# Delta-rule attention and a PReLU feed-forward on one core: another order for the first two products of the second feed-forward matrix, and other places for the copies of even steps' rows

## The chip, the core and the metric

The kernel runs on one core of a Trainium2 chip. Its engines are TensorE (PE in the profile, its weight loads PEld), VectorE (DVE), ScalarE (ACT), GpSimd (POOL) and SyncE (SP, which issues DMAs). Each takes its own list of instructions, and waits on semaphores where it needs what another engine makes. The metric is the device time of one execution in microseconds; the times of a kernel are given as the median of several runs.

## The reference

A delta-rule attention over 4 batches, 8 heads, 768 tokens and 48 dimensions; its output, as 3072 tokens of 384 numbers, goes through a feed-forward block of width 2048 with a PReLU whose slope differs by column. All in 32-bit floats.

```python
k_n = k / (np.linalg.norm(k, axis=-1, keepdims=True) + 1e-06)
for t in range(S):
    kt, vt, bt = (k_n[:, :, t], v[:, :, t], beta[:, :, t, None])
    y[:, :, t] = np.einsum('bhd,bhde->bhe', q[:, :, t], state)
    v_old = np.einsum('bhde,bhd->bhe', state, kt)
    state = state + bt[:, :, :, None] * np.einsum('bhd,bhe->bhde', kt, vt - v_old)
...
x = np.ascontiguousarray(attn_out.transpose(0, 2, 1, 3)).reshape(B * S, H * D)
h = x @ w_in
g = np.maximum(h, 0.0) + alpha * np.minimum(h, 0.0)
return (g @ w_out).astype(np.float32)
```

## The kernel before

**Steps and chunks.** The tokens go in 12 chunks of 64. The attention of one chunk takes two steps, one for each pair of batches, so there are 24 steps; step n belongs to chunk n // 2. The recurrence within a chunk is solved with triangular inverses, which VectorE makes for four steps at a time by elimination (`eliminate`, a list of small pieces). The feed-forward of a chunk handles 256 tokens: the first product (`ffn_in`, line 996) takes the 2048 columns in 8 pairs of 128, six matmuls to a pair, all into one bank of PSUM; ScalarE then writes the Relu of the negated bank to `act` (line 1006), and two VectorE operations (line 1008), one for each half of the pair, turn it into the PReLU. An fp32 matmul leaves two records in the profile.

**The second product.** From chunk 2 to chunk 7 it is `ffn_out_fast`: instead of eight products of 128 x 192 blocks with eight operand tiles each, seven (Winograd's form), on sums of blocks of `act` (`operand_sums`, VectorE, line 950; the second half of them is issued during the first product, two tiles apart) and sums of blocks of the weights. Each product runs its eight tiles in a row (`product`), into the next bank that `ps_ffn` hands out. The first product, of blocks (0, 0), is copied to `u` by ScalarE (line 1084); the second is added to it by VectorE (line 1081), and so on. Tile i of the first two products is pair i of `act`, so that their last tile is the last thing that the PReLU makes. From chunk 8 on other functions are used for both products: `ffn_in_fast` (lines 1219 to 1267), in which four shared matmuls of a pair go to one bank that ScalarE copies out (line 1248) before the next pair's may be written, and `ffn_out_faster` (line 1313).

**Order of the work.** The lists of all engines are written out by hand. A step from `JOINED` (6) on is: `burst_a` (outputs and next state of the step before, the keys through the state of this one: lines 840, 857, 802 on TensorE; then on VectorE the new state, line 865, `turn_y`, line 881, and `r`, line 812, and `a_t`, line 521); a first stretch; `turn_round`; a second stretch; `burst_b` (solve and the next steps' inverses: lines 784, 827, 733; VectorE's `u`, line 831; ScalarE's copies, line 745); a third stretch. In a stretch, `weave` interleaves feed-forward pieces (a piece is one matmul of `ffn_in`, two of `ffn_out_fast`) with pieces of other lists: each list (pieces, count, start) has its pieces spread evenly from its start to the stretch's end, at equal positions the list named first goes first:

```python
    def stretch(n, blocks, share, later, *gens, soon=0.5):
        gens = [(*x, 0.0) for x in (*gens, (part(tail, n), n))]
        gens += [(part(blocks, share), share, 0.3), (each(later), len(later), soon)]
```

In odd steps from 13 on the stretches hold 12, 18 and 12 feed-forward pieces (12, 16 and 12 in steps 9 and 11). A chunk has 48 + 28 = 76, which is what two steps hold, so each chunk's second product begins in the third stretch of an odd step: chunk 3's in step 9, chunk 7's in step 17.

**Banks.** PSUM has 8 banks. Up to step 7 three pairs of them serve the attention and two single banks (`p_ffn`) the feed-forward; at step `NARROW` (8) `banks(2, 2)` makes it two pairs and four single banks (`p_ffn` and `p_more`), and `len(ffn_banks)` becomes 4.

**Turning the attention's output.** The feed-forward needs it transposed (`xts`, two buffers). From step 8 to 22 this is done without TensorE: `turn_y(n - 1)` in `burst_a(n)` transposes 32 x 32 blocks on VectorE into `z`, and `rows_y` has 16 ScalarE copies (line 894) that put the blocks' rows in place. For odd steps n - 1 all 16 go to the first stretch of step n, from 0.4 of it on; for even ones, 8 to the second and 8 to the third stretch of step n.

Of the kernel before, what the change touches and what calls it, by code (L numbers as in the profile page):

```python
# [44 lines left out]
def kernel(  # L45
# [11 lines left out]
    nc = tc.nc  # L57

    B, H, S, D = q.shape
    DM = H * D  # L60
# [14 lines left out]
    doubles, big, ffn_banks = ExitStack(), [], []  # L75
# [25 lines left out]
    def ps_ffn():  # L101
        turn[0] = (turn[0] + 1) % len(ffn_banks)
        return ffn_banks[turn[0]]
# [79 lines left out]
    def load_v(n):  # L183
        if n < N:
            v_raw[n] = work.tile([128, H, D], FP32, name="v_raw", bufs=3)
            fetch(v, n, v_raw[n])
# [298 lines left out]
    def now(pieces):  # L485
        for x in pieces:
            x()
# [561 lines left out]
    def ffn_out_fast(c):  # L1049


        gss.pop(c)
        later = operand_sums(1)
        o = [work.tile([128, DM], FP32, name="o_sb") for _ in range(2)]
        left, right_ = slice(0, DM // 2), slice(DM // 2, DM)
        u = [work.tile([128, DM // 2], FP32, name=f"u{i}", bufs=1) for i in (2, 3)]

        def product(x, w):
            p = ps_ffn()[:, 0 : DM // 2]
            for i in range(FP):  # L1060
                nc.tensor.matmul(p, x(i), w(i), start=(i == 0), stop=(i == FP - 1))  # L1061
                if i % 2 == 1:
                    next(later, None)
                    if i < FP - 1:
                        yield
            return p

        def operand(f, u):
            return lambda i: act[:, i, f, u * 128 : (u + 1) * 128]

        def sum_(x):
            return lambda i: sums[:, i, x]

        def weight(f, v):
            return lambda i: w_half[:, i, f, v]

        def w_sum_(x):
            return lambda i: w_sum(i, x)

        def add(to, x, p):  # L1080
            nc.vector.tensor_tensor(out=to, in0=x, in1=p, op=ALU.add)

        p = yield from product(operand(0, 0), weight(0, 0))
        nc.scalar.copy(u[0], p)
        yield
        p = yield from product(operand(1, 0), weight(1, 0))
        add(o[0][:, left], u[0], p)
        yield
        for _ in later:
            assert False  # L1090
        assert summed.count(0) == summed.count(1) == 4
        p = yield from product(sum_(1), w_sum_(1))
        add(u[0], u[0], p)
        yield
        p = yield from product(lambda i: act[:, i, 0, 128:256], w_sum_(2))
        add(u[1], u[0], p)
        yield
        p = yield from product(sum_(0), w_sum_(0))
        add(o[0][:, right_], u[0], p)
        add(o[1][:, right_], u[1], p)  # L1100
        yield
        p = yield from product(sum_(2), weight(1, 1))
        add(o[0][:, right_], o[0][:, right_], p)
        store(c, 0, o[0])
        yield
        p = yield from product(operand(1, 1), w_sum_(3))
        add(o[1][:, left], u[1], p)
        store(c, 1, o[1])
        yield
# [296 lines left out]
    def is_turned(n):  # L1406
        return NARROW <= n < N - 1

    def burst_a(n):

        soon, later = [], []
        if n > NARROW:
            b = asked_in.pop()
            y, z = b[:, :, G * C : G * C + WY], b[:, :, 0:WY]
        else:
            b = ps_big()
            y, z = b[:, :, 0:WY], b[:, :, WY : 2 * WY]
        if n > JOINED:
            soon += outputs(n - 1, y)
            soon += next_state(n - 1, z)  # L1420
            if is_turned(n - 1):
                soon.append(lambda: turn_y(n - 1))
            later.append(lambda: load_late(n + 1))
        if n < N:
            p = ps_big()
            y = ps_big()[:, :, 0:WY] if n < NARROW else None
            soon += through_state(n, p[:, :, 0 : G * (D + C)], y)
            if n < JOINED + 2:
                soon += between_1(n + 1, b[:, :, 2 * WY : 2 * WY + G * HB])
            if n == JOINED:  # L1430
                soon += grams(n + EARLY, big[-1][:, :, WY : WY + G * C])
                later.append(lambda: squares(n + EARLY + 1))
            later.append(lambda: load_v(n + 3))
        now(soon)
        return later

# [264 lines left out]
    n = 12  # L1701
# [199 lines left out]
    for n in range(JOINED, N):  # L1901
        if n == NARROW:
            banks(2, 2)
        fill, share = FILL.get(n, FILLS[n % 2]), PIECES_OF.get(n, TURNS[n % NJ])
        extra = [[], [], []]
        if n == JOINED:
            place(n + 1, (0,))
            extra[1] = [(weight_sums(1, 0, 3), 3)]
            extra[2] = [(weight_sums(0, 3, 4), 1)]
        elif n == JOINED + 1:  # L1910
            extra[0] = [(weight_sums(1, 3, 4), 1, 0.6), (placing(n + 1, (1, 2, 3)), PLACING)]

        later = burst_a(n)
        if is_turned(n - 1):
            if n % 2:
                rows = rows_y(n - 1)
                extra[1].append((part(rows, 8), 8))
                extra[2].append((part(rows, 8), 8))
            else:
                extra[0].append((rows_y(n - 1), 16, 0.4))  # L1920
        stretch(fill[0], blocks, share[0], later, *extra[0], *put_off)
        put_off = []
        later = turn_round(n)
        if n == JOINED:
            extra[1].append((placing(n + 1, (1, 2, 3)), PLACING))
        stretch(fill[1], blocks, share[1], later, *extra[1], soon=0.2)
        m, ends = (n + 6) // NJ, n % NJ == 2
        if ends and n > JOINED:
            for _ in blocks:
                assert False  # L1930
            place(n + 2, (0,))
        later = burst_b(n) + [lambda: scale_v(n + 1)]
        if NARROW <= n < N - 2:
            later.append(lambda: turn_q(n + 2))
        if n == JOINED:
            stretch(fill[2], blocks, share[2], later, *extra[2])
            for _ in blocks:
                assert False
            place(n + 2, (0,))
            place(n + 3, (0,))  # L1940
            blocks = eliminate(m)
        else:
            if ends:
                blocks = eliminate(m) if m < N // NJ else iter(())
            after = [(placing(n + 2, (1, 2, 3)), PLACING)]
            if n % NJ != 1:
                after.append((placing(n + 3, (0,)), 1))
            if n >= LATE:
                put_off, after = after, []
            stretch(  # L1950
                fill[2], blocks, share[2], later, *after, *extra[2], soon=0.1 if n >= LATE else 0.5
            )
# [34 lines left out]
```

## Time and profile before

| | us |
|---|---|
| median of 3 runs | 651.65 |
| lowest, highest | 651.61, 652.92 |
| the profiled execution | 652.41 |
| its span, first to last instruction | 650.69 |

The profile's times are microseconds from the start of the span. A row of a timeline has its start, its length, engine, line, operation, tiles written and read, shape and count (successive equal instructions are merged), and in brackets the time that the engine sat idle before it and what ended that. Engines are strictly ordered lists; a wait of one instruction is a wait of everything behind it on its engine. The length of a matmul is modelled: they overlap, so that a run of them is read by the distance between starts.

In 40 equal slices of the span VectorE, ScalarE and GpSimd stand so (busy tenths, 9 is 90% or more):

```
DVE  4976998967999888858978857968967668567383
ACT  5887565345453344635544634435447356354140
POOL 6001211010000000001000000000035043062250
```

Lines 996, 1061 and 1313, the feed-forward products up to chunk 7 and the second one after it, are the largest groups of TensorE; of ScalarE it is line 894 with 64.4 us in 240 copies.

### The profile page before, as it was taken

Reading aid. Unit: us, or ns where it says so; the run is one execution under the profiler, and the core shown is the slowest. Engines: PE = TensorE matmul, PEld = TensorE weight load, DVE = VectorE, ACT = ScalarE, POOL = GpSimd, SP = SyncE. Lnnn points to the kernel's source line nnn. Section 1 sums busy time; section 2 is a strip of 40 time slices with the busy share of each in tenths; the row PEclk is TensorE's granted clock in tenths of the full one; section 3 lists DMA queues with packets and bytes.
Section 4 is the critical chain, followed back from the end, with each engine's and each line's share of the span. In section 5 each row is a group of like instructions: output and inputs, shape, how many; then the busy total and the mean of one; then the engine's idle time right before and its main releaser. Section 6 shows DMA issues by size and latency. Waiting matters only on the chain.

```text
span 650.7 us, 21683 instructions
## 1 busy us (share of the span) xinstructions
PE 629.2 (97%) x9154; PEld 552.3 (85%) x9154; DVE 498.2 (77%) x1205; ACT 313.1 (48%) x824; POOL 93.3 (14%) x204
## 2 busy tenths in 40 slices
PE   6999999999999998999999999999999999999997
PEld 4688888557788987988988888988989989999997
DVE  4976998967999888858978857968967668567383
ACT  5887565345453344635544634435447356354140
POOL 6001211010000000001000000000035043062250
PEclk9999999999999999999999999999999999999999
DMA  7957835211353242242243121121220210100000
GB/s 119 297 132 167 232 68 147 62 37 37 51 79 49 45 73 34 38 71 44 37 64 50 26 48 30 31 43 28 39 54 12 50 27 3 37 2 2 25 1 25
DMA packets 145969, 39.27 MB, mean 60 GB/s; under 512 B 139040, under 2 KB 142256, under 8 KB 145872
## 3 DMA queue, kind: packets, MB, share of 16 engines
q1 hardware_dynamic: 144000, 37.40, 28.2%
q8 instruction: 72, 1.18, 0.8%
q10 hardware_dynamic: 1872, 0.49, 0.4%
q14 instruction: 25, 0.20, 0.1%
HBM read 33.14 MB, written 4.72 MB: 58 GB/s over the span
## 4 chain that ended last, share of the span: by engine, by line
PE 71%; DVE 13%; ACT 5%; SPq 4%; DMA 3%; issue 2%; POOL 1%; ACTq 0%; DVEq 0%; POOLq 0%
PE p_ffn L1061 9%; PE p_ffn L996 8%; PE p_more L1061 7%; PE p_more L1313 7%; PE p_ffn L1039 6%; PE p_more L1229 4%; PE p_more L996 4%; PE p_ffn L1313 3%; PE p_ffn L1219 3%; DVE act L1008 3%; PE p_ffn L1224 2%; SPq L153 2%; PE p_pair L733 2%; PE p_pair L1480 2%; PE p_pair L802 2%
## 5 line engine op out<-in xcount | busy, mean ns | idle before, releaser
L996 PE MATMUL p_ffn<-xt,w_in 128*128 128x256 f32 x528 | 124.1, 384 | 2.4 <-DVE act L1008 1.8
L996 PEld LDWEIGHTS p_ffn<-xt,w_in 128*128 128x128 f32 x528 | 97.4, 190 | 17.5 <-ACT wgt L718 1.6
L894 ACT COPY xt<-z 32x96 f32<-32x96 f32 x240 | 64.4, 268 | 25.7 <-DVE z L881 22.6
L996 PE MATMUL p_more<-xt,w_in 128*128 128x256 f32 x240 | 55.7, 382 | 0.0
L745 ACT COPY inv<-p_pair 32x256 f32<-32x256 f32 x40 | 14.5, 362 | 84.7 <-DVE u L831 83.9
L599 DVE TENSOR_TENSOR block<-block,prod 128x30 f32<-128x30 f32 (+9 forms) x150 | 49.8, 332 | 5.1
L1253 POOL TENSOR_TENSOR k_t<-k_t 128x128 f32<-128x128 f32 (+1 forms) x48 | 28.9, 601 | 166.6 <-ACT k_t L1248 164.0
L996 PEld LDWEIGHTS p_more<-xt,w_in 128*128 128x128 f32 x240 | 44.9, 190 | 6.3
L593 DVE TENSOR_TENSOR prod<-block 128x30 f32<-128x30 f32 (+9 forms) x150 | 48.5, 324 | 1.2
L418 POOL TENSOR_TENSOR beta_t<-beta_t,rec 128x8 f32<-128x8 f32 x24 | 6.1, 255 | 276.5 <-DVE rec L412 267.5
L1008 DVE SCALAR_TENSOR_TENSOR act<-act,al_t,p_ffn 128x256 f32<-128x256 f32 x72 | 31.2, 475 | 17.6 <-ACT act L1006 17.6
L1006 ACT ACTIVATE act<-p_ffn 128x512 f32<-128x512 f32 x36 | 21.4, 595 | 36.7 <-PE p_ffn L996 36.6
L1061 PE MATMUL p_ffn<-w_out,act 128*128 128x192 f32 x160 | 28.1, 329 | 3.1 <-DVE act L1008 3.1
L1253 POOL TENSOR_TENSOR block<-block 128x128 f32<-128x128 f32 (+1 forms) x48 | 28.0, 582 | 15.5 <-ACT block L1248 13.0
L1061 PEld LDWEIGHTS p_ffn<-w_out,act 128*128 128x128 f32 x160 | 26.2, 190 | 4.1 <-DVE act L1008 3.7
L1219 PE MATMUL p_ffn<-xt,w_in 128*128 128x256 f32 x96 | 29.3, 387 | 0.0
L831 DVE TENSOR_TENSOR u<-p_pair,wgt 128x384 f32<-128x384 f32 x24 | 13.2, 553 | 18.0 <-PE p_pair L733 17.1
L1008 DVE SCALAR_TENSOR_TENSOR act<-act,al_t,p_more 128x256 f32<-128x256 f32 x40 | 17.3, 472 | 11.7 <-ACT act L1006 11.7
L1061 PE MATMUL p_more<-w_out,act 128*128 128x192 f32 x128 | 22.5, 328 | 2.8 <-DVE act L1008 2.8
L812 DVE TENSOR_TENSOR r<-v_raw,p_pair 64x192 f32<-64x192 f32 (+1 forms) x66 | 23.3, 353 | 2.3 <-PE p_pair L802 1.2
L1061 PEld LDWEIGHTS p_more<-w_out,act 128*128 128x128 f32 x128 | 20.9, 190 | 3.5 <-DVE act L1008 3.4
L554 ACT COPY same<-right 32x256 f32<-32x256 f32 x29 | 11.7, 403 | 22.7 <-DVE right L507 19.1
(254 smaller groups left out, 1473.1 us busy)
## 6 DMA issues: line engine op xcount, KB each, us to landing
w_out<-in_moe_w_in_dram SPq DMA_DIRECT2D x10, 512.0 KB, 5.1
v_raw<-in_v_dram SPq DMA_DIRECT2D x48, 96.0 KB, 2.7
kl<-in_k_dram SPq DMA_DIRECT2D x96, 48.0 KB, 2.4
out_dram<-o_sb SPq DMA_DIRECT2D x90, 48.0 KB, 1.6
space_out<-in_moe_w_out_dram SPq DMA_DIRECT2D x11, 384.0 KB, 4.5
ke_last<-in_k_dram SPq DMA_DIRECT2D x25, 96.0 KB, 3.2
qp<-in_q_dram SPq DMA_DIRECT2D x64, 32.0 KB, 2.2
w_out<-in_moe_w_out_dram SPq DMA_DIRECT2D x5, 384.0 KB, 4.5
```

The costliest lines, as they stand in the source:

```text
L593: nc.vector.tensor_tensor(out=prod, in0=r[:, 0:j, j : j + 1].to_broadcast([128, j, n]), in1=r[:, j : j + 1, j + 1 : HB].to_broadcast([128, ...
L599: nc.vector.tensor_tensor(out=r[:, 0:j, j + 1 : HB], in0=r[:, 0:j, j + 1 : HB], in1=prod, op=ALU.add)
L812: nc.vector.tensor_tensor(out=r[to, a], in0=v_in[to, a], in1=p[own, a, :, 0:D], op=ALU.subtract)
L894: nc.scalar.copy(to[quad(r), u, bp, t], z[quad(2 * t + u), r])
L996: nc.tensor.matmul(p_h[:, i], w_in[:, t, (f + i) * 128 : (f + i + 1) * 128], xt[:, t], start=(t == 0), stop=(t == KT - 1),)
L1008: nc.vector.scalar_tensor_tensor(out=g[:, i], in0=g[:, i], scalar=al_t[:, f + i : f + i + 1], in1=p_h[:, i], op0=ALU.mult, op1=ALU.add,)
L1039: nc.tensor.matmul(p_o[u], gs[f // 2][:, f % 2, u * 128 : (u + 1) * 128], w_out[:, f], start=(f == 0), stop=(f == FT - 1),)
L1061: nc.tensor.matmul(p, x(i), w(i), start=(i == 0), stop=(i == FP - 1))
L1219: nc.tensor.matmul(p[:, f * 256 : f * 256 + 256], w(2, f), xt[:, 2], start=True, stop=False)
L1229: nc.tensor.matmul(q[:, j], a, b, start=True, stop=True)
L1253: nc.gpsimd.tensor_tensor(out=dst, in0=a, in1=b, op=ALU.add)
L1313: nc.tensor.matmul(p, x(i), w(i), start=(i == 0), stop=(i == FP - 1))
```

## The change

It has two parts. In `ffn_out_fast`, with more than two banks for the feed-forward, the first two products are opened together: six tiles of the first, six of the second, the last two of the first, its copy to `u`, the last two of the second, its addition. The banks are handed out in the same order, and the count of pieces (28) stays. `some` is `product`'s loop over a given range of tiles; it still takes a piece of `operand_sums` after each second tile. With two banks the old order remains.

In odd steps n (whose rows are those of the even step n - 1) `turn_y` is issued at the end of `burst_a`, behind the pieces of `through_state` (`r` and `a_t`), and no longer ahead of them. The 16 row copies go 6 to the first stretch from 0.5 of it on, 2 to the second and 8 to the third from 0.3 on. In even steps nothing changes.

```diff
-        def product(x, w):
-            p = ps_ffn()[:, 0 : DM // 2]
-            for i in range(FP):
+        def some(p, x, w, which):
+            for i in which:
                 nc.tensor.matmul(p, x(i), w(i), start=(i == 0), stop=(i == FP - 1))
                 if i % 2 == 1:
                     next(later, None)
                     if i < FP - 1:
                         yield
+
+        def product(x, w):
+            p = ps_ffn()[:, 0 : DM // 2]
+            yield from some(p, x, w, range(FP))
             return p
...
+        if len(ffn_banks) > 2:
+            a, b = (
+                (ps_ffn()[:, 0 : DM // 2], operand(f, 0), weight(f, 0)) for f in range(2)
+            )
+            yield from some(*a, range(FP - 2))
+            yield from some(*b, range(FP - 2))
+            yield from some(*a, range(FP - 2, FP))
+            nc.scalar.copy(u[0], a[0])
+            yield
+            yield from some(*b, range(FP - 2, FP))
+            add(o[0][:, left], u[0], b[0])
+            yield
+        else:
+            p = yield from product(operand(0, 0), weight(0, 0))
+            nc.scalar.copy(u[0], p)
+            yield
+            p = yield from product(operand(1, 0), weight(1, 0))
+            add(o[0][:, left], u[0], p)
+            yield
...
-            if is_turned(n - 1):
+            if is_turned(n - 1) and n % 2 == 0:
                 soon.append(lambda: turn_y(n - 1))
             later.append(lambda: load_late(n + 1))
         if n < N:
...
             later.append(lambda: load_v(n + 3))
+        if is_turned(n - 1) and n % 2:
+            soon.append(lambda: turn_y(n - 1))
         now(soon)
...
                 rows = rows_y(n - 1)
-                extra[1].append((part(rows, 8), 8))
-                extra[2].append((part(rows, 8), 8))
+                extra[0].append((part(rows, 6), 6, 0.5))
+                extra[1].append((part(rows, 2), 2))
+                extra[2].append((part(rows, 8), 8, 0.3))
```

More of the change, by code (lines that the diff above doesn't have):

```diff
@@ L1081, in add @@
             nc.vector.tensor_tensor(out=to, in0=x, in1=p, op=ALU.add)
[L1083 to L1088, printed above, removed]
+        if len(ffn_banks) > 2:
[17 more added lines that the diff above has]
+            yield
         for _ in later:
```

## The prediction, made before the changed kernel was built or timed

> **What bounds the kernel now.** I read the page first, then the answer for line 1061 (all matmuls of the second feed-forward product), then the timelines of TensorE, ScalarE and VectorE around each of its waits.
>
> ```profile
> PE 629.2 (97%) x9154; PEld 552.3 (85%) x9154; DVE 498.2 (77%) x1205; ACT 313.1 (48%) x824; POOL 93.3 (14%) x204
> ...
> PEclk9999999999999999999999999999999999999999
> ```
>
> From the answer for line 1061:
>
> ```profile
> L1061 PE MATMUL p_more<-w_out,act x128: 326/326/430, 225.2 to 472.2; 128*128 128x192 f32 x128
> ...
> its engine sat idle before it (us, times) until:
>   DVE act L1008: 12.9, 8
> ```
>
> TensorE sets the time: busy for 97% of the span at full granted clock, every other engine has room. So only an idle stretch of TensorE is worth anything, and line 1061 has one kind: matmuls waiting for `act`. The 12.9 counts weight loads and matmuls both; the matmuls' part, with the rows ahead of each wait (start, length, then the idle time in brackets):
>
> ```profile
> 256.02 2.44 PE L1061 MATMUL p_ffn<-w_out,act 128*128 128x192 f32 x14
> 260.72 3.19 PE L1061 MATMUL p_ffn<-w_out,act 128*128 128x192 f32 x18 [2.25 <-DVE act L1008]
> ...
> 306.22 2.44 PE L1061 MATMUL p_more<-w_out,act 128*128 128x192 f32 x14
> 309.91 0.59 PE L1061 MATMUL p_more<-w_out,act 128*128 128x192 f32 x2 [1.25 <-DVE act L1008]
> ...
> 355.42 2.44 PE L1061 MATMUL p_more<-w_out,act 128*128 128x192 f32 x14
> 359.39 3.19 PE L1061 MATMUL p_more<-w_out,act 128*128 128x192 f32 x18 [1.53 <-DVE act L1008]
> ...
> 404.42 2.44 PE L1061 MATMUL p_ffn<-w_out,act 128*128 128x192 f32 x14
> 407.68 0.59 PE L1061 MATMUL p_ffn<-w_out,act 128*128 128x192 f32 x2 [0.82 <-DVE act L1008]
> ...
> 452.25 5.36 PE L1061 MATMUL p_ffn<-w_out,act 128*128 128x192 f32 x32
> ```
>
> A matmul leaves two records. Each block is chunks 3, 4, 5, 6, 7 in turn; 14 records are operand tiles 0 to 6, and the wait is always at tile 7. Chunk 7 has none. Its 32 unbroken records give the pitch: (5.36 - 0.33) / 31 = 0.162 us. Record 15 would start 14 x 0.162 = 2.27 after the first, so the waits cost 260.72 - 256.02 - 2.27 = 2.43, then 1.42, 1.70 and 0.99: **6.54 us in all**, a little over the idle column, because a resumed matmul also loses its overlap.
>
> Why tile 7 is late, in chunk 4 (ScalarE rows, then VectorE):
>
> ```profile
> 305.58 0.73 ACT L745 COPY inv<-p_pair 32x256 f32<-32x256 f32 x2 [3.29 <-DVE u L831]
> 306.33 0.74 ACT L745 COPY mid<-p_pair 32x256 f32<-32x256 f32 x2
> 307.08 0.51 ACT L704 ACTIVATE inv<-inverse,which 128x256 f32<-128x256 f32 x1
> 307.50 0.39 ACT L707 COPY diag<-turned 128x256 f32<-128x256 f32 x1
> 307.89 0.83 ACT L894 COPY xt<-z 32x96 f32<-32x96 f32 x3
> 308.75 0.60 ACT L1006 ACTIVATE act<-p_more 128x512 f32<-128x512 f32 x1
> ...
> 305.00 0.55 DVE L831 TENSOR_TENSOR u<-p_pair,wgt 128x384 f32<-128x384 f32 x1
> 309.38 0.87 DVE L1008 SCALAR_TENSOR_TENSOR act<-act,al_t,p_more 128x256 f32<-128x256 f32 x2 [2.57 <-ACT act L1006]
> ```
>
> VectorE's `u` comes at the end of its queue, four copies of ScalarE wait for it, and the Relu of pair 7 stands behind them and three row copies. Relu, then the first of the two line-1008 operations (half of 0.87), then TensorE goes on.
>
> **Part one, the order of the products.** No instruction is added or removed. From four banks on, the first product's tiles 0 to 5 are followed by the second's 0 to 5, then 6 and 7 of each. Chunk 2 still has two banks (its first products are all `p_ffn`), so chunks 3 to 7 change. Tile 7's matmul becomes record 27 instead of 15: due 26 x 0.162 = 4.21 after the start, at 260.23, 310.43, 359.63 and 408.63, against releases at 260.72, 309.91, 359.39 and 407.68. Alone, this leaves 0.49 us in chunk 3 and nothing elsewhere. Is alternating between two open banks free? The last chunks' product (line 1313) already does it in this order:
>
> ```profile
> 545.29 4.39 PE L1313 MATMUL p_more<-w_out,act 128*128 128x192 f32 x26
> 549.87 1.24 PE L1313 MATMUL p_more<-w_out,act 128*128 128x192 f32 x6 [0.19 <-DVE act L1267]
> ```
>
> (4.39 - 0.33) / 25 = 0.162, the same pitch, so I take nothing for it; bounds 0 both ways, since the rows agree to a nanosecond. [...]
>
> The copy of `u` (line 1084) and the add behind it are issued six matmuls, about 2 us, later. What is late next is the third product's second half, which needs the second of the `sums` operations of VectorE:
>
> ```profile
> 261.81 0.69 DVE L950 TENSOR_TENSOR sums<-sums,act 128x512 f32<-128x512 f32 x1
> ...
> 266.89 1.57 PE L1061 MATMUL p_more<-more,sums 128*128 128x192 f32 x8
> ```
>
> It is ready at 262.50 and would be wanted at 266.89 - 2.4 = 264.5: 2 us to spare in the worst chunk, so no new wait there.
>
> **Part two, the copies.** Of even steps' 16 row copies, 6 go to the second half of the first stretch, 2 to the second, 8 to the third from 0.3 on; before it was 8 and 8 from the start of the second and third. By the order in which `weave` interleaves lists of these lengths, the Relu of pair 7 loses the row copies ahead of it: three in chunks 4 to 6 (0.83 us, row above), one in chunk 3. With its 0.27 less, chunk 3's release is 260.45: 0.22 us remain. Gain so far 6.54 - 0.22 = **6.32**.
>
> The price is paid in the first stretch. `turn_y` now follows `r` and `a_t` on VectorE, and the six copies wait for its `z`, with Relus queued behind them. Step 11, the worst:
>
> ```profile
> 294.41 0.58 DVE L881 STREAM_TRANSPOSE z<-y 128x384 f32<-128x384 f32 x1
> 295.02 1.09 DVE L812 TENSOR_TENSOR r<-v_raw,p_pair 128x192 f32<-128x192 f32 x3
> 296.14 0.69 DVE L521 TENSOR_TENSOR a_t<-p_pair,minus 128x512 f32<-128x512 f32 x1
> ...
> 299.03 0.86 DVE L1008 SCALAR_TENSOR_TENSOR act<-act,al_t,p_more 128x256 f32<-128x256 f32 x2
> ...
> 294.50 0.21 ACT L408 ACTIVATE norm<-norm 128x8 f32<-128x8 f32 x1
> ...
> 296.23 0.60 ACT L1006 ACTIVATE act<-p_more 128x512 f32<-128x512 f32 x1 [0.93 <-PE p_more L996]
> ```
>
> `z` would end at 296.7. Then on ScalarE: one copy (0.27), the Relu of pair 3 (0.60), five copies (1.4), two norm operations (0.45), one copy, and the Relu of pair 4 ends near 300.3. VectorE wants it at 299.03, so it falls 1.3 us behind, and carries that to `u`. TensorE does not see it directly: pair 4's bank is next written at 306.22. But chunk 4's release becomes 309.91 - 0.83 + 1.3 = 310.38 against 310.43: still covered, by a hair. In the other odd steps to 17 the same reckoning gives less, and idle time takes it up.
>
> In steps 19 and 21 it is ScalarE's copy out of the shared bank (line 1248) that stands behind five copies:
>
> ```profile
> 487.25 0.40 ACT L718 COPY wgt<-wgt 64x4 f32<-64x4 f32 x2
> 487.99 0.58 ACT L1248 COPY k_t<-p_more 128x512 f32<-128x512 f32 x1 [0.34 <-ACT wgt L718]
> ...
> 489.27 0.39 PE L1229 MATMUL p_more<-xt,w_in 128*128 128x128 f32 x2
> ...
> 486.75 0.49 PE L1229 MATMUL p_more<-xt,w_in 128*128 128x128 f32 x2 [0.57 <-ACT block L1248]
> ```
>
> It would start at 487.65 + 5 x 0.277 = 489.03 and end at 489.61; TensorE, which needs that bank at 489.27, waits some 0.4 us. The last row shows that it does wait for this copy where that is late. Twice: **-0.8**, bounds 0 and 2 x 1.39 = 2.8 (all five copies felt). Step 23 has no `wgt` copies there and just fits.
>
> In the third stretch of steps 19 and 21 copies leave the way of the Relu whose VectorE operation ends the 0.19 wait at 549.87 (and its twin): 0 to 0.35 us each with the lost overlap, I take 0.25, **+0.5**.
>
> **Sum:** 6.3 + 0.5 - 0.8 = 6.0 us. The profiled execution took 652.41 with a span of 650.69; its like after the change 646.4, span 644.7. The median of the runs, 651.65, lies 0.76 below it: **645.7**.
>
> **Rivals.**
> *The stall only moves.* VectorE, at 77%, is what was late; TensorE arriving 1 to 2.4 us earlier meets the next operation of its queue. For it: chunk 4's release comes out only 0.05 us ahead of its need. Against: the 2 us spare at `sums`, and VectorE sat idle 2.57 us while it waited for the Relu. If half of the 6.3 comes back as new waits, or step 11's lag and those like it eat two chunks' gain (1.4 + 1.7), some 3 us are left: 648.6.
> *The copies in front hold TensorE: slower.* One mechanism: ScalarE takes its queue in order, so a copy that waits for `z` holds the Relu or line-1248 copy behind it until the bank is missing on TensorE. In favour:
>
> ```profile
> L894 ACT COPY xt<-z x240: 253/268/272, 247.0 to 593.6; 32x96 f32<-32x96 f32 x120
> ...
>   DVE z L881: 22.6, 8
> ```
>
> ScalarE already stands 22.6 us in 8 waits for `z`. If in all eight odd steps the later `z` (1.09 + 0.69 = 1.8) passed to TensorE, that is 14.2 us against 6.8 gained: 659. It decides only once a Relu is more than about 5 us late (300.3 to 306.22 in step 11); I find at most 3.5.
> *The change doesn't reach the waits.* Were the bank count read before the switch to four, the old branch would run and only the copies would act: Relu 0.83 earlier, so 0.27 + 3 x 0.83 = 2.8 less 1.3 for step 11, less 0.8, plus 0.5 = 1.2 us: 650.5. Against: `p_more` is in use by line 1061 from 225.2 on, 30 us before chunk 3.
> [...]
>
> **How the numbers follow.** Forecast 0.72; the stall moves 0.16; slower by the copies 0.05; not reached 0.06; clock 0.01. The forecast's own range is 644.4 (all 6.54, twice 0.35, no price: 7.2) to 647.7 (price 2.8). With the second case the range is **644.4 to 649.2**, which leaves out about 0.15. Faster by over 0.2% (1.3 us, about what a measurement of this kernel can tell) has the first two: 0.88; within 0.2%: 0.06; slower: 0.06.
>
> **What would show it.** Right: line 1061 without waits for `act` in chunks 4, 5, 6, and at most a few tenths in chunk 3; unbroken blocks of 28 to 32 records there; the Relu of pair 7 directly behind the four line-745 copies and line 704; a new wait of some 0.4 us before line 1229 in steps 19 and 21; `z` after `a_t` in odd steps. Wrong: line 996 waiting for `act` or a bank in odd steps' first two stretches; waits before `sums`; a wait at tile 7 in chunk 4 of over 0.3 us, which would say that step 11's lag was sized too small.

## The result

| | before, us | after, us |
|---|---|---|
| median of 4 runs each | 652.24 | 647.27 |
| lowest, highest | 651.61, 652.92 | 645.59, 647.38 |
| profiled execution, its span | 652.41, 650.69 | 645.59, 643.87 |

The ratio is 0.9918, 95% interval 0.9897 to 0.9939: the change makes the kernel faster by 5.0 us in the medians, where 6.0 were predicted, and 647.27 lies in the predicted range. The change was timed twice more, on two chips, as experiments e3 and e9: 645.72 against 653.62 (ratio 0.9893, 0.9870 to 0.9916) and 646.11 against 651.70 (0.9912, 0.9897 to 0.9927). The two profiled executions lie 6.82 us apart.

### The profile page after: what moved, and what is told of

Its sections match the earlier page's. It is cut to its first block, busy times and chain, and to the rows that moved or that the text cites. A ratio compares the mean times of both kernels' runs of the same rounds, so it can differ in the third digit from the quotient of the medians.

```text
span 643.9 us, 21686 instructions
## 1 busy us (share of the span) xinstructions
PE 628.6 (98%) x9154; PEld 552.2 (86%) x9154; DVE 497.9 (77%) x1205; ACT 312.8 (49%) x824; POOL 92.5 (14%) x204
## 3 DMA queue, kind: packets, MB, share of 16 engines
q8 instruction: 72, 1.18, 0.8%
## 4 chain that ended last, share of the span: by engine, by line
PE 87%; DVE 6%; DMA 2%; ACT 1%; issue 1%; SPq 1%; POOL 1%; ACTq 0%; DVEq 0%; POOLq 0%
PE p_ffn L996 13%; PE p_ffn L1060 9%; PE p_more L996 8%; PE p_more L1329 8%; PE p_more L1060 8%; PE p_ffn L1039 7%; PE p_more L1245 4%; PE p_ffn L1329 3%; PE p_ffn L1235 3%; PE p_pair L733 2%; PE p_ffn L1240 2%; PE p_pair L802 2%; PE p_pair L840 2%; PE p_pair L1498 2%; PE p_pair L501 2%; PE p_pair L827 2%
## 5 line engine op out<-in xcount | busy, mean ns | idle before, releaser
L1283 DVE SCALAR_TENSOR_TENSOR act<-k_t,al_t,act 128x256 f32<-128x256 f32 x32 | 19.4, 645 | 3.6 <-ACT k_t L1279 3.5
```

## The profile after

From the page of the changed kernel, the busy times and the granted clock:

```profile
PE 628.6 (98%) x9154; PEld 552.2 (86%) x9154; DVE 497.9 (77%) x1205; ACT 312.8 (49%) x824; POOL 92.5 (14%) x204
...
PEclk9999999999999999999999999999999999999999
```

From the answer for line 1060 (1061 before: the matmuls of the second product):

```profile
its engine sat idle before it (us, times) until:
  DVE act L1008: 0.2, 1
```

TensorE's work is the same to 0.6 us, in a shorter span, and the 12.9 us in 8 waits for `act` have become 0.2 in one. The timeline of TensorE, at the first two products of chunks 3, 4 and 5:

```profile
255.46 5.52 PE L1060 MATMUL p_ffn<-w_out,act 128*128 128x192 f32 x32
...
303.29 2.11 PE L1060 MATMUL p_more<-w_out,act 128*128 128x192 f32 x12
305.24 2.11 PE L1060 MATMUL p_ffn<-w_out,act 128*128 128x192 f32 x12
307.19 0.84 PE L1060 MATMUL p_more<-w_out,act 128*128 128x192 f32 x4
307.87 0.81 PE L1060 MATMUL p_ffn<-w_out,act 128*128 128x192 f32 x4
...
351.76 5.36 PE L1060 MATMUL p_more<-w_out,act 128*128 128x192 f32 x32
```

Chunk 4 shows the new order as it is: 12 records of one bank, 12 of the other, 4, 4, with no bracket for idle time. Chunk 5 is as long as chunk 7 was before, which did not wait; chunk 3 is 5.52 - 5.36 = 0.16 us longer, what is left of its wait.

Why tile 7 now comes in time in chunk 4 (ScalarE, then VectorE):

```profile
303.95 0.73 ACT L745 COPY inv<-p_pair 32x256 f32<-32x256 f32 x2 [4.88 <-DVE u L831]
...
305.86 0.39 ACT L707 COPY diag<-turned 128x256 f32<-128x256 f32 x1
306.27 0.60 ACT L1006 ACTIVATE act<-p_more 128x512 f32<-128x512 f32 x1
...
306.90 0.87 DVE L1008 SCALAR_TENSOR_TENSOR act<-act,al_t,p_more 128x256 f32<-128x256 f32 x2 [1.73 <-ACT act L1006]
```

The Relu stands directly behind the copies that wait for `u`, with no row copy between. Half of the line-1008 pair ends near 306.90 + 0.87/2 = 307.34; tile 7 is due 4.21 after 303.29, at 307.50. By these rows the margin is 0.16 us.

The two kernels issue the same matmuls in the same steps, so where the time went can be read from the start of a step's first line-840 (or 784) matmul in the two timelines:

| TensorE reaches | before, us | after, us | apart | gained since the row above |
|---|---|---|---|---|
| step 9 (line 840) | 238.79 | 238.23 | -0.56 | 0.56, from the start to step 9 |
| step 10 | 265.14 | 262.21 | -2.93 | 2.37, chunk 3 |
| step 12 (line 784) | 329.37 | 324.94 | -4.43 | 1.50, chunk 4 |
| step 13 | 336.46 | 332.80 | -3.66 | -0.77, line 733 in step 12 |
| step 14 | 362.51 | 357.06 | -5.45 | 1.79, chunk 5 |
| step 16 | 410.81 | 404.26 | -6.55 | 1.10, chunk 6 |
| step 19 (line 784) | 495.11 | 488.71 | -6.40 | -0.15, line 1245 in step 19 |
| step 20 | 504.26 | 497.59 | -6.67 | 0.27, third stretch of step 19 |
| step 21 (line 784) | 541.89 | 535.36 | -6.53 | -0.14, line 1245 in step 21 |
| step 22 | 551.05 | 544.23 | -6.82 | 0.29, third stretch of step 21 |

The losses are visible in TensorE's timeline. In step 12, in the middle of a run of 32 x 32 matmuls:

```profile
326.35 0.19 PE L733 MATMUL p_pair<-inv,mid 32*32 32x32 f32 x1
327.11 0.18 PE L733 MATMUL p_pair<-inv,mid 32*32 32x32 f32 x1 [0.57 <-issue]
```

"issue" means that the engine waited for nothing that the profile shows. In step 19, TensorE's rows and then ScalarE's:

```profile
480.08 0.49 PE L1245 MATMUL p_more<-xt,w_in 128*128 128x128 f32 x2 [0.44 <-ACT block L1264]
...
482.39 0.38 PE L1240 MATMUL p_ffn<-k_t,w_in 128*128 128x128 f32 x2
482.77 0.49 PE L1245 MATMUL p_more<-xt,w_in 128*128 128x128 f32 x2
...
492.11 5.55 PE L1329 MATMUL p_more<-w_out,act 128*128 128x192 f32 x32
...
480.45 0.54 ACT L894 COPY xt<-z 32x96 f32<-32x96 f32 x2
481.00 0.40 ACT L718 COPY wgt<-wgt 64x4 f32<-64x4 f32 x2
481.41 0.83 ACT L894 COPY xt<-z 32x96 f32<-32x96 f32 x3
482.15 0.57 ACT L1264 COPY k_t<-p_more 128x512 f32<-128x512 f32 x1
```

The 0.44 is an old wait (0.57 before). The new one shows as a distance between starts: 482.77 - 482.39 = 0.38, where this pair of lines runs at 0.22 in the kernel with the old places of the copies (e1). Three copies, not five, stand between `wgt` and the copy of the bank.

## The experiments

All were timed beside the kernel before on the same chip: e1 to e4 on one (before 653.62, 17 runs), e5 to e8 on a second (652.88, 17 runs), e9 to e12 on a third (651.70, 11 runs). Diffs are against the changed kernel.

**e1: the order of the products alone**, copies and `turn_y` as before.

```diff
-            if is_turned(n - 1) and n % 2 == 0:
+            if is_turned(n - 1):
                 soon.append(lambda: turn_y(n - 1))
...
-                extra[0].append((part(rows, 6), 6, 0.5))
-                extra[1].append((part(rows, 2), 2))
-                extra[2].append((part(rows, 8), 8, 0.3))
+                extra[1].append((part(rows, 8), 8))
+                extra[2].append((part(rows, 8), 8))
```

> The new order of the first two products alone; the copies of even steps' rows and turn_y as before. Theory (the order takes the waits, by making the last tile due 12 records later): chunks 4 to 6 without a wait at the last tiles, chunk 3 with 0.49 us (release 260.72 against due 260.23 in the old clock); steps 19 and 21 keep the 0.2 us wait before the second product's last tiles and have none behind the copy of the shared bank. 6.05 us less than before, so 0.5 us more than the full change, too little to tell from it by time. Rival (the copies do it, the order only opens banks): 2 us or less below the kernel before, waits at the last tiles in chunks 3 to 6 about as before.

Measured: 646.49 us (645.00 to 649.32), ratio 0.9908 (0.9883 to 0.9934). Chunk 3's two products in TensorE's timeline:

```profile
255.36 4.39 PE L1060 MATMUL p_ffn<-w_out,act 128*128 128x192 f32 x26
260.05 1.24 PE L1060 MATMUL p_ffn<-w_out,act 128*128 128x192 f32 x6 [0.30 <-DVE act L1008]
```

The first wait is now at record 27, as the order says, and costs 260.05 - 255.36 - 4.21 = 0.48 (0.49 predicted). Chunks 4 to 7 have none. The order alone brings nearly all of the gain.

**e2: the copies alone**, the products in their old order (`ffn_out_fast` as before the change).

```diff
-        if len(ffn_banks) > 2:
...
-        else:
...
+        p = yield from product(operand(0, 0), weight(0, 0))
+        nc.scalar.copy(u[0], p)
+        yield
+        p = yield from product(operand(1, 0), weight(1, 0))
+        add(o[0][:, left], u[0], p)
+        yield
```

> The copies of even steps' rows and turn_y moved as in the change; the order of the products as before. Theory: the waits at tile 7 stay, shorter by the copies that leave the way: chunk 3 2.43 - 0.27 = 2.2 us, chunk 4 1.42 - 0.83 + 1.3 = 1.9 (longer, step 11's lag reaches it because nothing covers it now), chunk 5 0.9, chunk 6 0.2; 0.2 us waits at the shared bank in steps 19 and 21; together about 1.5 us less than before. Rival (the copies do it): 4 us or more below the kernel before, chunk 4's wait shorter than 1 us.

Measured: 650.16 us (647.61 to 652.65, 12 runs), ratio 0.9954 (0.9935 to 0.9973). TensorE's timeline at tile 7 of chunks 3, 4 and 5:

```profile
256.45 2.44 PE L1061 MATMUL p_ffn<-w_out,act 128*128 128x192 f32 x14
260.88 4.87 PE L1061 MATMUL p_ffn<-w_out,act 128*128 128x192 f32 x18 [2.00 <-DVE act L1008]
...
308.06 2.44 PE L1061 MATMUL p_more<-w_out,act 128*128 128x192 f32 x14
312.24 0.59 PE L1061 MATMUL p_more<-w_out,act 128*128 128x192 f32 x2 [1.73 <-DVE act L1008]
...
357.74 2.44 PE L1061 MATMUL p_more<-w_out,act 128*128 128x192 f32 x14
360.73 3.19 PE L1061 MATMUL p_more<-w_out,act 128*128 128x192 f32 x18 [0.55 <-DVE act L1008]
```

By starts (less 2.27) the waits are 2.16, 1.91 and 0.72, against 2.43, 1.42 and 1.70 before. The waits of chunks 3 and 5 are shorter by 0.27 and 0.98, what the copies ahead of the Relu cost (one of 0.27, three of 0.83) and a little more; chunk 4's wait is longer by 0.49, which is step 11's lag (1.3) less the three copies (0.83), 0.47. So the second part of the change has the two effects that were predicted, close to their sizes. In the times, e2 is 3.5 us below before by the medians, where some 1.5 were expected; but 12 of the 17 executions of before and only 2 of e2's 12 had a mean granted clock below 0.9985. Among the others the medians are 651.10 and 650.08, 1.0 apart.

One row was not expected: 18 records took 4.87 us and not 3.19. The windows of the same execution, whose columns are busy time of the engines, then the granted clock (before the DMA share and GB/s):

```profile
261.00:262.00 1.00, 1.00 (x4) 1.00 (x5) 0.93 (x3) 0.72 (x4) 0.00 (x0) 0.60 0.00 0
262.00:263.00 1.00, 1.00 (x4) 1.00 (x4) 0.96 (x3) 0.98 (x3) 0.00 (x0) 0.50 0.00 0
263.00:264.00 1.00, 1.00 (x5) 1.00 (x5) 1.00 (x3) 0.94 (x4) 0.00 (x0) 0.50 0.00 0
264.00:265.00 1.00, 1.00 (x6) 1.00 (x5) 0.96 (x4) 0.94 (x5) 0.00 (x0) 0.69 0.00 0
```

Directly behind the wait TensorE has half its clock: 0.40 + 0.50 + 0.50 + 0.31 = 1.71 us of clock lost in some 3.4 us, the 4.87 - 3.19 = 1.68 of the row. The profiles of before and after have no such stretch there.

**e3: the change again**, on this chip, unaltered.

> The changed kernel once more, beside the other three on the same chip, so that they are compared with it: 5 to 6.5 us below the kernel before. If the 0.6 us stop of TensorE inside line 733 near 327 us in its first profile is an accident of that execution and no part of the change, it is absent here or stands elsewhere; if it belongs to the change it stands at the same place.

Measured: 645.72 us (644.54 to 647.13), ratio 0.9893 (0.9870 to 0.9916). In its profile chunk 3 loses 0.31, and the stop of 0.58 in line 733 stands at 326.17 again. It isn't chance of one execution.

**e4: one tile left for later instead of two, and no copies in the first stretch** (`turn_y` at its old place).

```diff
-            yield from some(*a, range(FP - 2))
-            yield from some(*b, range(FP - 2))
-            yield from some(*a, range(FP - 2, FP))
+            yield from some(*a, range(FP - 1))
+            yield from some(*b, range(FP - 1))
+            yield from some(*a, range(FP - 1, FP))
...
-            yield from some(*b, range(FP - 2, FP))
+            yield from some(*b, range(FP - 1, FP))
...
-            if is_turned(n - 1) and n % 2 == 0:
+            if is_turned(n - 1):
...
-                extra[0].append((part(rows, 6), 6, 0.5))
-                extra[1].append((part(rows, 2), 2))
+                extra[1].append((part(rows, 8), 8))
```

> A version by the theory: only the last tile of the two products is left for later (due 28 records after the start instead of 26), turn_y stands as before, no copies in the first stretch of odd steps, 8 in the second, 8 in the third from 0.3 on. Theory: no wait at the last tiles in any of chunks 3 to 7 (chunk 3's 0.2 us goes too), no wait behind the shared bank at the second of its two places in steps 19 and 21 (0.17 us each go), VectorE's 1.2 us idle time in step 11 before the operation on pair 4 gone; 0.5 us below the full change, inside its noise by time, visible in the trace. Rival (the 6 early copies are needed to clear the third stretch): the Relu of pair 7 later than in the full change, waits at the last tiles come back.

Measured: 643.80 us (643.01 to 644.46), ratio 0.9864 (0.9841 to 0.9887), the fastest of this chip's five. TensorE's timeline:

```profile
255.08 5.40 PE L1060 MATMUL p_ffn<-w_out,act 128*128 128x192 f32 x32
...
478.91 0.49 PE L1245 MATMUL p_more<-xt,w_in 128*128 128x128 f32 x2 [0.57 <-ACT block L1264]
```

Chunk 3 is unbroken, and in step 19 only the old wait of before is left. The waits account for some 0.3 + 2 x 0.15 = 0.6 us of the 1.9 to e3; the rest was open until e9 to e12.

**e5: the new order in chunk 3 only, and e6: in all but chunk 3**, both with the copies of before. They ask whether chunk 3's wait, the longest, is what brings the half-clock stretch.

```diff
-        if len(ffn_banks) > 2:
+        if len(ffn_banks) > 2 and c == 3:
```

> The new order in chunk 3 alone, copies as before: only the longest wait, 2.43 us, is taken away but for 0.46. Theory (a wait of some 2 us can also bring a stretch of half clock, 3.4 us long, behind it, as in the profile of the copies alone behind the 2.0 us wait of chunk 3; it does so in most runs of the kernel before and not in all, and that is why runs differ): runs at granted clock 1.000 are 2 us below those of the kernel before; runs with a lower clock become rare, 1 or 2 in 6 against 12 in 17, so that the median falls by some 4 us. Rival (the stretches of half clock come from elsewhere, the start-up for one): the median falls by 2 us and runs below 1.000 stay as frequent as before.

```diff
-        if len(ffn_banks) > 2:
+        if len(ffn_banks) > 2 and c != 3:
```

> The new order in chunks 4 to 7, chunk 3 and the copies as before: waits of 1.42, 1.70 and 0.99 us are taken away, the one of 2.43 stays. Theory: runs at clock 1.000 are 4.1 us below those of the kernel before; lower clocks stay about as frequent as in the kernel before (2 runs in 3), a half-clock stretch standing behind chunk 3's wait near 260 us where the profile caught one. Rival (stretches of half clock are independent of chunk 3's wait): as rare as in the run with the order alone.

Measured: e5 650.29 us (648.60 to 653.37, 12 runs), ratio 0.9962 (0.9945 to 0.9978); e6 648.95 (646.43 to 650.77, 6 runs), ratio 0.9935 (0.9914 to 0.9957). In the profiles each has the waits that were left to it and no other; e6 in chunk 3:

```profile
258.30 3.19 PE L1060 MATMUL p_ffn<-w_out,act 128*128 128x192 f32 x18 [2.27 <-DVE act L1008]
```

e5's 2.6 us lie between the two theories. The mean granted clock was below 0.9985 in 3 of its 12 executions, in 4 of e6's 6, and in 10 of the 17 of before. Among the other executions e5 is 651.65 - 650.19 = 1.5 us below before (2 expected) and e6, with two such executions, 651.65 - 647.4 = 4.2 (4.1 expected). The counts agree with chunk 3's wait as a cause of such stretches, but e2, whose wait of 2.0 us was kept, has 2 of 12, and e6's own profile has none behind the 2.27. How often a wait brings one stays open.

**e7: all 16 copies in the first stretch**, from 0.4 on: the dose at which the rival "the copies in front hold TensorE" should decide.

```diff
-                extra[0].append((part(rows, 6), 6, 0.5))
-                extra[1].append((part(rows, 2), 2))
-                extra[2].append((part(rows, 8), 8, 0.3))
+                extra[0].append((part(rows, 16), 16, 0.4))
```

> The full change, but all 16 copies of an even step's rows in the first stretch from 0.4 of it on, as odd steps' have it: the dose of the slower rival. Theory (ScalarE takes its queue in order; the copies reach TensorE once what they hold up is later than its cover): waits at tile 7 of 1.3 us in chunk 3, 2.4 in chunk 4, 0.6 in chunk 5, 0.4 in chunk 6; waits behind the shared bank of 2.6 us in steps 19 and 21 and 2.4 in step 23; 11 us above the full change and 5 above the kernel before, with half-clock stretches behind the longer waits. Rival (copies in front never reach TensorE, the banks cover them): within 1 us of the full change.

Measured: 660.79 us (659.90 to 661.48, 5 runs), ratio 1.0118 (1.0098 to 1.0138): slower than before. The waits in TensorE's timeline (line 501 in steps 9, 11 and 13, tile 7 in chunk 3, then the shared bank in steps 19, 21 and 23):

```profile
252.55 0.69 PE L501 MATMUL p_pair<-k_t 48*64 48x64 f32 x32 [1.24 <-DVE k_t L478]
...
260.74 1.24 PE L1060 MATMUL p_ffn<-w_out,act 128*128 128x192 f32 x6 [0.60 <-DVE act L1008]
...
302.38 0.69 PE L501 MATMUL p_pair<-k_t 48*64 48x64 f32 x32 [2.08 <-DVE k_t L478]
...
351.89 0.69 PE L501 MATMUL p_pair<-k_t 48*64 48x64 f32 x32 [0.75 <-DVE k_t L478]
...
489.76 0.80 PE L1245 MATMUL p_more<-xt,w_in 128*128 128x128 f32 x2 [2.40 <-ACT k_t L1264]
...
540.10 0.49 PE L1245 MATMUL p_more<-xt,w_in 128*128 128x128 f32 x2 [2.41 <-ACT k_t L1264]
...
588.92 0.49 PE L1245 MATMUL p_more<-xt,w_in 128*128 128x128 f32 x2 [1.90 <-ACT k_t L1264]
```

At the shared bank the waits came where and as long as they were expected (2.6, 2.6, 2.4 against 2.40, 2.41, 1.90). In the earlier steps most of the delay came back not at tile 7 but at line 501, for which VectorE transposes `k_t` in its queue behind the delayed work. At tile 7 there is less than was expected: by the starts 0.78 us in chunk 3, 0.27 in chunk 4, none in chunk 5 and 0.41 in chunk 6 (1.3, 2.4, 0.6 and 0.4 expected). The six other waits make 10.8 us; behind the two of 2.4 us stands a half-clock stretch each, here two windows of the first:

```profile
490.00:491.00 1.00, 1.00 (x6) 1.00 (x7) 0.60 (x2) 0.90 (x3) 0.84 (x3) 0.50 0.00 0
491.00:492.00 1.00, 1.00 (x5) 0.97 (x5) 1.00 (x3) 0.08 (x1) 0.64 (x1) 0.50 0.00 0
```

With e2's 1.7 us for each of the two and 1.5 at tile 7 that is 15.7 us, of which the change itself has some 0.5; e7 stands 660.79 - 646.11 = 14.7 above the change (on another chip), where 11 were expected.

**e8: the last four tiles left for later.** If the order works only by the time at which tile 7 falls due, it must now work less well: the first tile 7 stands at record 23 again.

```diff
-            yield from some(*a, range(FP - 2))
-            yield from some(*b, range(FP - 2))
-            yield from some(*a, range(FP - 2, FP))
+            yield from some(*a, range(FP - 4))
+            yield from some(*b, range(FP - 4))
+            yield from some(*a, range(FP - 4, FP))
...
-            yield from some(*b, range(FP - 2, FP))
+            yield from some(*b, range(FP - 4, FP))
```

> The full change with the last four tiles of the first two products left for later instead of two: tile 7's matmul is record 23, due 3.56 us after the start instead of 4.21. No part of the computation changes. Theory (what counts is how late tile 7 is due): a wait of 0.9 us in chunk 3 and of 0.5 in chunk 4, none in 5 to 7; 1.2 us above the full change. Rival (any order with both banks open is as good): no such waits, equal to the full change.

Measured: 647.18 us (645.46 to 648.14), ratio 0.9906 (0.9887 to 0.9925). TensorE's timeline in chunks 3 and 4:

```profile
254.56 3.74 PE L1060 MATMUL p_ffn<-w_out,act 128*128 128x192 f32 x22
259.01 1.89 PE L1060 MATMUL p_ffn<-w_out,act 128*128 128x192 f32 x10 [0.72 <-DVE act L1008]
...
307.39 0.59 PE L1060 MATMUL p_more<-w_out,act 128*128 128x192 f32 x2 [0.43 <-DVE act L1008]
```

Waits come back at record 23 (259.01 - 254.56 - 22 x 0.162 = 0.89) and in chunk 4, none after: as the due times say. The sum over the execution is too small to be told from the change by its time.

**e9 to e12: what e4's lead is made of.** Two edits crossed on one chip: e9 is the change, e10 has one tile left for later, e11 the copies and `turn_y` of e4 with two tiles, e12 is e4 again. Their diffs are the halves of e4's.

> The change itself, as one of four kernels that cross two edits on one chip: two tiles or one left for later, and the change's places of copies and turn_y or those with none in the first stretch. Both theories expect some 646 us, ratio near 0.990, and a stop of TensorE of 0.4 to 0.6 us in line 733 near 327 us that nothing in the profile explains.

> The change with one tile of each of the first two products left for later instead of two. Tile 7 is then first wanted two tile pairs later, 28 x 0.162 = 4.54 us after the start and no longer 4.21, so chunk 3's rest of 0.2 to 0.3 us goes. Theory (the sum of waits is all there is): 0.2 us less than the change. Rival (the order of the instructions also sets stops that no wait explains, as the one in line 733): 0.6 to 1.5 us less, and no stop in line 733.

> The change with the copies and turn_y placed otherwise: turn_y ahead of r and a_t as before, no copy in the first stretch, 8 in the second from its start, 8 in the third from 0.3 on; two tiles left for later as in the change. Theory (the sum of waits): the new waits of 0.16 us in steps 19 and 21 go, chunk 3 keeps 0.3 us: 0.3 us less than the change. Rival (copies that wait for z in the first stretch cost TensorE more than its waits show, through the line-1006 Relus behind them): 1 to 2 us less.

> The kernel with both edits, one tile left for later and no copies in the first stretch, again on this chip; it took 643.80 us, ratio 0.9864, where the change took 645.72. If it is the better version the two repeat with some 2 us between them. Theory (the sum of waits): 0.5 us between them, and the larger distance was chance. Rival: 2 us, and the two single edits share it.

| | two tiles | one tile |
|---|---|---|
| 6 copies in the first stretch | e9: 646.11 (644.76 to 646.81), ratio 0.9912 (0.9897 to 0.9927) | e10: 646.00 (645.27 to 646.47), ratio 0.9912 (0.9898 to 0.9926) |
| none in the first stretch | e11: 644.25 (643.72 to 645.52), ratio 0.9889 (0.9872 to 0.9907) | e12: 644.66 (643.43 to 645.11), ratio 0.9889 (0.9872 to 0.9907) |

One tile or two makes no difference that these runs can tell, though chunk 3's block is 5.65 us long in e9 and 5.40 in e12. The places of the copies make 1.3 to 1.9 us, five to seven times what the waits of steps 19 and 21 explain (0.26, below). In the profiles of e9 and then e10 the list of TensorE's waits (total, times, longest) has:

```profile
PE p_pair L733 <- issue: 0.9, 1, 0.9
```

```profile
PE p_pair L733 <- issue: 0.7, 1, 0.7
```

e11 has no such stop in TensorE's list; the largest of the kind there is 0.5 in line 857. From the line-784 matmuls of step 12 to the line-840 ones of step 13 e9 takes 333.26 - 325.11 = 8.15 us and e11 331.74 - 324.57 = 7.17: 0.98 less, and another 0.26 less in steps 19 and 21; the other 0.5 of the 1.8 us between the two profiles stands before step 9, up to which the two do the same work. So the rival had the size right; its means, Relus behind the copies, isn't what the profiles show. They show the stop in line 733, which the last section takes up. e11 and e12, with 0.9889, beat both kernels, and e4 with 0.9864 on the first chip says the same.

## Why the prediction was right

**TensorE bounds, and line 1061's wait for `act` is what the change reaches.** Right. e1 and e2 change one part each, and the waits move by the amounts that the prediction read from the rows.

**The order is worth 6.32 us in chunks 3 to 6.** Right, a little small: 2.37, 1.50, 1.79 and 1.10 make 6.76. What is left in chunk 3 was put at 0.22 and is 0.16 (0.31 in e3, 0.29 in e9). The other 0.1 per chunk is a detail of the rows of before that the prediction passed over: its resumed block of 18 records took 3.19 us, where 0.33 + 17 x 0.162 = 3.08 would do.

**Alternating between two banks is free.** Right: chunk 5's block of 32 records took 5.36 us, as long as chunk 7's before, and the clock row stays at 9. The forecast's chances give 0.01 to the clock, and no run shows that alternating lowers it: the profiled executions of after, e1, e4 to e6 and e8 to e12 alternate and had a mean granted clock of 1.000; the half clock in e3 and e7 began near waits of 1.96 us in line 429 and of 2.40 and 2.41 in line 1245.

**Step 11 falls 1.3 us behind, and chunk 4 is covered by a hair.** Right in both. In ScalarE's and VectorE's timelines after:

```profile
293.80 0.27 ACT L894 COPY xt<-z 32x96 f32<-32x96 f32 x1 [5.04 <-DVE z L881]
293.98 0.58 ACT L1006 ACTIVATE act<-p_more 128x512 f32<-128x512 f32 x1
294.59 1.40 ACT L894 COPY xt<-z 32x96 f32<-32x96 f32 x5
...
296.75 0.60 ACT L1006 ACTIVATE act<-p_more 128x512 f32<-128x512 f32 x1
...
297.38 0.87 DVE L1008 SCALAR_TENSOR_TENSOR act<-act,al_t,p_more 128x256 f32<-128x256 f32 x2 [1.18 <-ACT act L1006]
```

The queue is the one that was written down: one copy, a Relu, five copies, the norms, one copy, the Relu for which VectorE stands 1.18 us. The margin was put at 0.05 and is 0.16 from half of the line-1008 pair on; but in the rows of before TensorE went on only some 0.1 us after that moment (309.91 against 309.38 + 0.87/2), so that by the prediction's reckoning it is 0.06.

**The price at the shared bank, -0.8.** The place was right, the size was not: 0.15 + 0.14 = 0.29. In step 19 that is 0.38 - 0.22 = 0.16 for the new wait and 0.11 of lost overlap behind it (the next pair starts 0.33 later, and 0.22 later in e1), less 0.13 by which the old wait is shorter. The mis-sized step is "it would start at 487.65 + 5 x 0.277": two of the five copies stand ahead of `wgt`, as the rows of step 19 show, where ScalarE had been idle for 487.25 - 486.69 = 0.56 before, and only three behind it.

**The third stretches of steps 19 and 21, +0.5.** Right: 0.27 + 0.29 = 0.56. Line 1329's 32 records take 5.55, with no idle time in the row of the matmuls, but still 0.19 more than an unbroken block's 5.36: a rest of the wait is left. e4, whose third stretch is the same, has that block in 5.54.

So the local terms make 6.76 - 0.29 + 0.56 = 7.03 against 6.0. Two things were not in the sum: the 0.77 lost in step 12 (the stop in line 733, 327.11 - 326.35 = 0.76 between two starts; it is in the profiles of e1, e3, e6, e7, e9 and e10 too), and 0.56 gained before step 9, where nothing was changed in what is computed and profiles of one kernel differ by as much (e3 and e9, both the change, stand 1.15 apart at step 9 already). 7.03 - 0.77 + 0.56 = 6.82.

**The medians.** The prediction carried the profiled execution's gain to the medians by 0.76 us, its distance from the median. After the change the profiled execution came out 0.8 below its forecast of 646.4, but it is the fastest of four, and the median lies 1.68 above it. That step, not the terms, makes the 1.6 us by which 645.7 missed. The upper end of the range, 649.2, stands above the 648.6 of its second case without a working; the result does not need it.

**The rivals.** "The stall only moves": no, the waits before `sums` and tile 7 did not come. "The change doesn't reach the waits": no; e2, which is that case, keeps the waits at tile 7 that the change has lost. It had been put 1.2 us below before, and is 1.0 below it among executions at full clock (3.5 by all). "The copies in front hold TensorE": not at six copies; e7 shows it at sixteen, 7.9 us above before where 7.4 had been worked out for the rival, though 4.1 us of its waits come at line 501, which the prediction did not look at.

## What to carry to other kernels

Where the last operand of a product is always the late one, let the next product's early operands stand between: the due time moves by their pitch (here 12 records of 0.162 us, 1.94 us) and costs no instruction, and in e1, which does this alone, no wait elsewhere was paid for it. Before something is put into the idle time of an engine with one queue, list what stands behind it there up to the first consumer on the bounding engine; here the sum of durations gave the delay well in step 11 (1.3 us, where VectorE stood 1.18), and too much in step 19 (0.4 us, where the wait was 0.16), where two pieces stood on the other side of a third. Try the parts alone: here one half of the second part, the copies in the first stretch with the later `turn_y`, costs more than it brings, and the versions without it (e11, e12) are 1.3 to 1.9 us faster.

## What was not expected of the hardware

**Half clock behind a wait of 2 us.** In e2 and e7 TensorE ran at 0.50 for some 3.4 us, beginning within 0.6 us of the end of waits of 2.00, 2.40 and 2.41 us, which costs some 1.7 us more than the wait. Not every such wait has one behind it: the profiles show none behind 2.25 us in before, 2.27 in e6, 2.08 and 1.90 in e7. And one stands where the change has no part, in e3's profile near the start:

```profile
15.69 1.92 PE L429 MATMUL p_pair<-ident,qp 128*112 128x128 f32 x8 [1.96 <-POOL same L550]
```

From 15 to 20 us the windows of 1 us there have a clock of 0.85, 0.50, 0.50, 0.50 and 0.94. That is all that e3's mean clock of 0.997 lacks, and the execution, with 644.65, was still below its kernel's median.

Of the kernel before, 12 of 17, 10 of 17 and 7 of 11 executions on the three chips had a mean clock below 0.9985; of the kernels whose longest wait at tile 7 is under 1 us and which have no other new wait over 1 us (after, e1, e3, e4, e8 to e12), 7 of 49. On the first two chips such executions of before were 2.8 and 1.9 us longer by the median (653.92 against 651.10, 653.57 against 651.65), on the third no longer (651.60 against 651.87). Among the executions at 0.9985 and over, the change gains 651.10 - 645.84 = 5.3 us on the first chip and 651.87 - 646.11 = 5.8 on the third, near the 6.0 that were predicted. That the gain by all executions was 7.9 us on the first chip, and 5.6 on the third, fits with this. That the stretches of before stood at chunk 3 is not shown: the one execution of before that has a trace ran at full clock, and e3's trace shows that a low mean can come from elsewhere.

**Stops of TensorE without a wait.** One stands in line 733 of step 12, at the same matmul in profiles on three chips: 0.35 us (e1) to 0.86 (e9) in the idle column, 0.54 to 1.05 between the two starts. Kernels with the new order have it (after, e1, e3, e6, e7, e9, e10), but not e4, e8, e11 and e12, nor before, e2 and e5, whose matmuls there are the same. Neither part of the change alone goes with it: e1 has it with the old copies and e8 lacks it with the new ones.

What the traces hold beside it is the transfer of instructions. The page of the changed kernel has it among the DMA queues (packets, MB, share):

```profile
q8 instruction: 72, 1.18, 0.8%
```

These are 72 transfers of 16384 bytes. The page does not say for which engine they are; that they bring TensorE's instructions is the author's estimate, from the times that follow. By the times of the DMA packets in the traces, each of the 37 stops that the timelines of TensorE's matmuls in the fourteen profiles put down to "issue" ends 1.2 to 1.6 us after the last of these transfers had landed (in after the 39th lands at 325.80, and the stop in line 733 ends at 327.11). The one for step 12, the 39th, lands 0.50 to 1.11 us after the step's first line-784 matmul in the seven profiles with the stop, and from 1.05 before it to 0.13 after it in the seven without. The stop, taken between starts, is as long as that time to within 0.2 us: 0.50 and 0.54 us in e1, 0.85 and 0.76 in after, 0.98 and 1.05 in e9, 1.11 and 0.93 in e10. So TensorE seems, by this estimate, to have run out of instructions there. No run moved a transfer on purpose, and why it starts later in some of these kernels stays open. The stop is the larger part of what e11 gains on e9 in the profiles.
